# One queue for all transfers of the attention stage, expert weights in pieces of 256 KB, and the order of the parts written anew

## The chip, the core and the metric

The kernel runs on one core of a Trainium2 chip. The metric is the device time of one execution in microseconds (us). The kernel before takes 458.43 us (median of 3 runs, 458.0 to 460.66). Engines: TensorE (PE; its weight loads are PEld), VectorE (DVE), ScalarE (ACT), GpSimd (POOL). Transfers are issued from a queue of SyncE (SP) and from ACT's own instruction stream (ACTq in the rows).

## The reference, cut to what matters

Three stages follow each other: attention with a hash mask over 16 heads (2 batches of 8), a soft mixture of 8 experts, and a feed-forward layer with a sigmoid gate.

```python
# attention, per head: q, k, v are 768 x 64; proj is 64 x 6
mask = bucket(q @ proj > 0)[:, None] == bucket(k @ proj > 0)[None, :]
scores = where(mask, (q @ k.T) / 8, -1e9)
attn = softmax(scores) @ v              # 16 heads -> x: 1536 x 512
# experts: phi 512 x 32, w1 8 x 512 x 1024, w2 8 x 1024 x 512
logits = x @ phi
slots = softmax(logits, axis=0).T @ x   # 32 slots, 4 per expert
slot_out = relu(slots @ w1[e]) @ w2[e]
x = softmax(logits, axis=1) @ slot_out
# feed-forward: w_in 512 x 2048, w_out 2048 x 512, both float64
h = x @ w_in
out = (h * sigmoid(1.702 * h)) @ w_out  # float32, 1536 x 512
```

## The kernel before, in words

**Attention** works head by head (n = 0 to 15). For each head: `raw.n` loads q and k (128 x 768, 384 KB) into one of two buffers, `raw0` for even heads and `raw1` for odd ones; `bits.n` (PE, L370) projects them, `bits2.n` (DVE, L359) makes the bucket code `Bt`, and `bits3.n` moves it in four transfers of 48 KB into rows of the operand tile `QK2`. `hi2`, `hi1`, `hq` (ACT) and `lo1`, `lo2` (ACT and DVE, L341 and L347) split q and k into a high and a low part. `a.n.i` (PE L428, DVE L435) finds the row maxima, `mr.n` (PE, DVE) turns them into a row, and `ms.n` stores it (3 KB) into `QK2`. Then `c` (L478) and `s` (L486) make a block of scores on PE, ACT takes the exponential (L487) into `P`, POOL sums (L495), and `av` (L501) multiplies by v, which `v.n` loads (192 KB). The buffer of `raw.n` comes free when the last `lo2.(n-2)` has read it. The heads overlap: while one head's scores are made, the maxima of the next and the codes of the one after are under way.

Between them run parts of the later stages: `win.j` loads a 16th of w_in (512 KB), `w1.j` to `w3.j` narrow it to float32 in the one tile `wn`, and `w4.j` stores it to DRAM (256 KB, `win32`). `we.i` loads expert tile i (1 MB) for i = 0 to 13 into 14 reserved tiles, which nothing uses before. `spin` and `idle` are matmuls without a use that keep PE busy at the start.

**The order** is written out by hand: the string ATTENTION lists the parts (`c.3.2.0` is part c, head 3, key block 2, query half 0), a loop (L681 to L683) records them in that order, and each engine and queue does its own instructions strictly in that order, waiting where data or a buffer is not ready. A part does not wait for its turn in the string on another engine: SP runs ahead until one of its own instructions has to wait. MISC and XROWS assign buffers to parts in order of use.

**Queues before.** SP's queue carries the loads `raw`, `v`, `win`, `phi`, the moves `bits3` and the stores `ms` of heads 1 to 14. ACT's stream carries the 14 loads `we` (L205), the 16 stores `w4` (L656) and `ms.15` (L468), each between its computing instructions. Transfers share eight completion semaphores in turn, so that each one also waits for the one issued eight before it.

**After attention** the loads of expert tiles 14 to 31 stand in SP's queue (`more`, L730), the first nine of them (14 to 22) into memory that the attention stage gives back, the others into tiles that become free as `expert_in` (L935) and the loop at L975 use up experts 0, 1 and so on; then the tiles of w_out and of the narrowed w_in. The feed-forward stage (L1162 on) is one long row of matmuls.

Of the kernel before, what the change touches and what calls it, by code (L numbers as in the profile page):

```python
# [42 lines left out]
idle.0 hi1.0.0 spin.6 hi2.0.1 bits.0 lo.0.1 hi2.0.0 code.1.1 spin.2 code.1.0 code.0.0 hq.0 code.0.1 a0.0 bits.1 a0.5
a0.3 a0.4 lo.0.0 spin.1 a0.2 a0.1 hi1.0.1 a0.9 spin.1 a0.8 a0.6 c.0.0.0 raw.2 bits2.1 bits.2 hi2.1.0 mred.0 hi2.1.1
a0.10 mr0.0 a0.11 hi2.2.0 a0.7 bits3.1 mr1.0 lo.1.1 bits2.2 spin.1 hi2.2.1 spin.1 hi1.1.0 c.0.3.0 hi1.1.1 mred.1
s.0.0.0 a.1.0 spin.1 s.0.3.0 c.0.1.0 spin.1 vs.0 mr0.1 mr1.1 c.0.1.1 lo.1.0 w1.0 raw.3 v.1 a.1.1 c.0.2.0 spin.1 spin.1
s.0.1.0 p.0.1.0 s.0.1.1 spin.1 bits3.2 s.0.2.0 a.1.2 spin.1 c.0.4.0 spin.3 p.0.2.0 s.0.4.0 c.0.4.1 c.0.3.1 a.1.5
s.0.4.1 s.0.3.1 c.0.0.1 s.0.0.1 lo1.2.1 w2.0 hq.1 spin.2 c.0.5.1 a.1.4 c.0.2.1 w3.0 s.0.2.1 vs.1 av.0.0 av.0.1 p.0.1.1
a.1.3 c.0.5.0 s.0.5.1 hq.2 av.0.2 a.2.3 p.0.3.0 s.0.5.0 mr.1 av.0.3 c.1.0.0 lo2.2.1 w4.0 a.2.0 bits.3 win.1 p.0.4.0
av.0.4 hi2.3.0 ms.1 w1.1 hi2.3.1 bits2.3 a.2.1 s.1.0.0 bits3.3 w2.1 av.0.5 avo.0 p.0.2.1 c.1.0.1 p.0.3.1 s.1.0.1  # L50
p.0.4.1 a.2.2 mp.1 p.0.5.1 c.1.1.0 p.0.5.0 s.1.1.0 c.1.1.1 s.1.1.1 c.1.2.0 p.1.1.0 w3.1 s.1.2.0 c.1.3.0 s.1.3.0 w4.1
win.2 lo1.2.0 a.2.4 v.2 av.1.0 p.1.2.0 c.1.3.1 c.1.2.1 lo2.2.0 hi1.2.1 a.3.5 s.1.2.1 raw.4 we.0 av.1.1 s.1.3.1 c.1.4.0
p.1.1.1 a.2.5 p.1.2.1 w1.2 s.1.4.0 c.1.5.1 p.1.3.1 w2.2 av.1.2 mr.2 mp.2 ms.2 c.1.5.0 a.3.0 s.1.5.0 w3.2 s.1.5.1
bits.4 c.1.4.1 a.3.4 s.1.4.1 c.2.0.0 c.2.1.0 s.2.1.0 s.2.0.0 p.1.3.0 vs2.0 hi2.4.0 lo1.3.0 hq.3 c.2.0.1 vs.2 p.1.4.1
w4.2 bits2.4 win.3 s.2.0.1 a.3.3 av.1.3 av.1.4 p.1.5.1 c.2.2.0 p.1.4.0 c.2.1.1 bits3.4 p.1.5.0 lo1.3.1 a.3.1 nom.1
s.2.2.0 lo2.3.0 s.2.1.1 hi2.4.1 p.2.1.0 av.1.5 avo.1 c.2.3.1 hi1.3.1 a.3.2 c.2.2.1 s.2.2.1 c.2.3.0 s.2.3.0 sum.0 v.3
we.1 a.4.1 s.2.3.1 p.2.2.0 nom.0 av.2.0 lo2.3.1 av.2.1 av.2.2 w1.3 av.2.3 c.2.4.0 w2.3 we.2 p.2.1.1 mr.3 mp.3 c.2.4.1
s.2.4.1 c.2.5.0 raw.5 p.2.2.1 s.2.4.0 p.2.3.0 ms.3 w3.3 xtok.0 a.4.3 rec.0 s.2.5.0 we.3 c.2.5.1 s.2.5.1 xp.0 c.3.0.0
a.4.0 hi1.4.1 av.2.4 hi2.5.0 p.2.4.0 p.2.5.0 av.2.5 xn.0 bits.5 w4.3 lo1.4.0 c.3.1.0 p.2.3.1 p.2.4.1 s.3.1.0 bits2.5
bits3.5 a.4.5 s.3.0.0 c.3.0.1 s.3.0.1 win.4 xtok.1 avo.2 p.3.1.0 hq.4 raw.17 c.3.2.0 s.3.2.0 lo2.4.0 lo1.4.1 c.3.1.1  # L60
p.2.5.1 s.3.1.1 a.4.4 av.3.0 lo2.4.1 p.3.2.0 we.4 c.3.2.1 s.3.2.1 xp.1 c.3.3.0 hi2.5.1 a.4.2 xn.1 c.3.3.1 s.3.3.1
raw.6 vs.3 s.3.3.0 phi av.3.1 av.3.2 p.3.3.0 c.3.4.0 a.5.5 p.3.1.1 mp.4 p.3.2.1 s.3.4.0 c.4.4.0 c.3.4.1 s.3.4.1 mr.4
p.3.3.1 xT.0.0 c.3.5.0 s.3.5.0 a.5.0 lo1.5.0 p.3.4.1 bits.6 bits2.6 c.3.5.1 w1.4 c.4.2.0 ms.4 a.5.1 s.4.4.0 s.3.5.1
p.3.5.1 v.4 s.4.2.0 lo2.5.0 av.3.3 hi2.6.1 p.3.4.0 av.3.4 av.3.5 w2.4 hi1.5.1 a.5.2 bits3.6 c.4.1.0 avo.3 c.4.0.0 we.5
c.4.0.1 s.4.0.0 s.4.0.1 s.4.1.0 p.3.5.0 w3.4 vs2.1 a.5.3 c.4.1.1 s.4.1.1 c.4.3.0 lo1.5.1 s.4.3.0 c.4.4.1 p.4.1.0
av.4.0 win.5 p.4.1.1 hq.5 av.4.1 xT.0.1 c.4.3.1 lo2.5.1 a.5.4 s.4.3.1 lg.0 hi2.6.0 raw.7 sum.1 v.5 a.6.0 mr.5 c.4.5.0
p.4.2.0 c.4.2.1 s.4.2.1 s.4.5.0 raw.16 p.4.2.1 s.4.4.1 p.4.3.1 w4.4 rec.1 a.6.1 c.4.5.1 ms.5 av.4.2 bits.7 w1.5 vs.4
bits2.7 av.4.3 hi1.6.1 s.4.5.1 w2.5 hi2.7.1 bits3.7 nom.3 nom.2 c.5.1.1 c.5.0.0 w3.5 we.6 p.4.3.0 a.6.4 p.4.4.1 vs.5
hi2.7.0 w4.5 p.4.5.1 av.4.4 av.4.5 a.6.2 v.6 c.5.1.0 s.5.1.0 s.5.0.0 xtok.2 xtok.3 s.5.1.1 c.5.2.0 s.5.2.0 xp.2 xn.2
a.6.3 xp.3 avo.4 c.5.0.1 s.5.0.1 vs2.2 c.5.2.1 lo1.6.1 p.4.4.0 win.6 xn.3 lo2.6.1 mp.5 c.5.4.0 lo1.6.0 p.4.5.0 s.5.2.1  # L70
s.5.4.0 c.5.4.1 a.6.5 s.5.4.1 p.5.1.0 lo2.6.0 p.5.2.0 av.5.0 av.5.1 av.5.2 hq.6 p.5.1.1 a.7.0 c.5.3.1 c.5.5.0 raw.8
s.5.5.0 c.5.3.0 p.5.2.1 s.5.3.0 mr.6 s.5.3.1 xT.1.1 c.5.5.1 w1.6 a.7.1 s.5.5.1 av.5.3 p.5.3.1 av.5.4 bits.8 p.5.4.1
hi2.8.0 bits2.8 av.5.5 vs.6 c.6.0.0 hi1.7.1 ms.6 a.7.5 s.6.0.0 p.5.3.0 c.6.0.1 c.6.1.0 s.6.1.0 xT.1.0 p.5.4.0 s.6.0.1
w2.6 c.6.1.1 p.5.5.1 a.7.2 w3.6 bits3.8 p.5.5.0 hi2.8.1 avo.5 c.6.2.0 s.6.1.1 s.6.2.0 c.6.3.0 lg.1 lo1.7.0 a.7.3
lo2.7.0 p.6.1.0 s.6.3.0 p.6.1.1 nom.5 p.6.2.0 sum.2 v.7 lo1.7.1 win.7 c.6.2.1 c.6.4.0 s.6.2.1 s.6.4.0 hq.7 lo2.7.1
w1.7 nom.4 a.7.4 raw.9 p.6.2.1 mp.6 av.6.0 w4.6 av.6.1 vs.7 av.6.2 a.8.5 c.6.4.1 s.6.4.1 c.6.5.0 c.6.3.1 s.6.3.1 mr.7
s.6.5.0 p.6.3.1 c.6.5.1 w2.7 s.6.5.1 a.8.0 p.6.3.0 av.6.3 hi2.9.1 p.6.4.1 we.7 w3.7 bits.9 av.6.4 bits2.9 hq.8 a.8.4
ms.7 c.7.0.0 rec.2 c.7.1.0 s.7.0.0 s.7.1.0 xtok.4 a.8.1 lo1.8.0 lo2.8.0 c.7.0.1 hi1.8.1 p.7.1.0 s.7.0.1 av.6.5 avo.6
p.6.4.0 c.7.1.1 lo1.8.1 mp.7 c.7.2.0 s.7.2.0 w4.7 a.8.3 win.8 av.7.0 xp.4 s.7.1.1 c.7.2.1 xn.4 s.7.2.1 p.6.5.0 a.8.2
p.6.5.1 av.7.1 hi2.9.0 xtok.5 p.7.2.0 c.7.4.0 c.7.3.0 lo2.8.1 bits3.9 s.7.4.0 a.9.1 s.7.3.0 c.7.3.1 raw.10 p.7.1.1  # L80
p.7.2.1 mr.8 s.7.3.1 w1.8 xp.5 av.7.2 c.8.0.0 c.7.5.0 xn.5 p.7.3.0 p.7.4.0 a.9.5 s.7.5.0 av.7.3 ms.8 s.8.0.0 a.9.4
p.7.3.1 xT.2.0 c.7.5.1 w2.8 v.8 c.8.3.0 s.8.3.0 w3.8 c.7.4.1 s.7.4.1 s.7.5.1 hi2.10.0 a.9.0 vs2.3 lo1.9.0 c.8.2.0
c.8.0.1 s.8.0.1 lo2.9.0 av.7.4 av.7.5 w4.8 p.7.4.1 bits.10 bits2.10 p.7.5.1 hi2.10.1 xT.2.1 mp.8 c.8.1.0 c.8.3.1 hq.9
bits3.10 s.8.1.0 avo.7 s.8.2.0 p.8.1.0 a.9.3 lg.2 lo1.9.1 p.7.5.0 c.8.1.1 nom.6 s.8.1.1 a.9.2 c.8.2.1 p.8.1.1 s.8.3.1
p.8.2.0 hi1.9.1 s.8.2.1 av.8.0 p.8.3.0 c.8.5.0 c.8.4.0 lo2.9.1 mp.9 win.9 s.8.4.0 s.8.5.0 a.10.3 mr.9 w1.9 w2.9
c.8.4.1 av.8.1 av.8.2 sum.3 s.8.4.1 p.8.2.1 v.9 c.8.5.1 raw.11 w3.9 we.8 a.10.1 s.8.5.1 vs.8 c.9.1.0 ms.9 p.8.3.1
# [1167 lines left out]
```

## Time and profile before

| | |
|---|---|
| median of the runs | 458.43 us (458.0 to 460.66) |
| profiled execution | 462.48 us, span 460.5 us |
| busy in the span | PE 96%, DVE 66%, ACT 62%, POOL 47% |
| attention stage | about 0 to 259 us |
| experts | about 259 to 300 us |
| feed-forward | about 300 to 460 us |
| transfers | 75 MB, mean 163 GB/s |

All times inside the execution are us from the start of the span. PE is called busy for as long as a matmul of it is under way, and these overlap, so that 96% says little; where it waited is seen in the idle time in front of an instruction. The chain of waits is followed back from the last instruction, so that a transfer in it is one for which everything else waited.

### The profile page before, as it was taken

To read this page: it belongs to the slowest core of one execution; us is meant where nothing else is said; L and a number is where in the kernel's file an instruction comes from. 1 tells how busy PE (TensorE), PEld (TensorE's weight loads), DVE (VectorE), ACT (ScalarE), POOL (GpSimd) and SP (SyncE) were. 2 spreads that over 40 slices of the span, in tenths; PEclk is the share of its full clock that TensorE was granted. 3 is DMA by queue.
4 is the path that set the end of the run, shared out by engine and by line. 5 is a ranking of instruction groups with operands and counts; after the bars stand their busy time and mean duration, and the time that the engine had idled before them with its cause. 6 is when DMAs were issued, how large, how long until landed. Compare 5 with 4: busy or idle time off the path is not lost.

```text
span 460.5 us, 7059 instructions
## 1 busy us (share of the span) xinstructions
...
## 2 busy tenths in 40 slices
...
GB/s 158 102 84 228 88 325 236 205 217 70 192 142 103 140 145 204 145 171 148 106 226 264 426 381 426 388 419 422 81 0 1 1 0 139 0 1 68 0 2 68
DMA packets 22023, 75.08 MB, mean 163 GB/s; under 512 B 3210, under 2 KB 8804, under 8 KB 16612
## 3 DMA queue, kind: packets, MB, share of 16 engines
...
q14 instruction: 16, 0.13, 0.1%
...
## 4 chain that ended last, share of the span: by engine, by line
PE 70%; DMA 15%; DVE 7%; ACT 5%; issue 2%; POOL 0%; SPq 0%; ACTq 0%; DVEq 0%; POOLq 0%
PE o L1130 28%; PE av L501 9%; PE b L478 6%; DMA raw<-in_qk 6%; DMA w<-in_w 6%; PE a L428 6%; PE b L486 6%; PE h L1102 2%; PE bp L370 2%; DVE MX L435 2%; DVE QK L347 2%; ACT P L487 1%; DMA QK<-mr 1%; PE xtp L583 1%; DMA win<-wn 1%
## 5 line engine op out<-in xcount | busy, mean ns | idle before, releaser
L495 POOL TENSOR_TENSOR Ps<-Ps,P 128x384 f32<-128x384 f32 x120 | 119.2, 1007 | 38.9 <-ACT P L487 36.3
L487 ACT ACTIVATE P<-b 128x384 f32<-128x384 f32 x192 | 87.1, 491 | 42.6 <-PE b L486 40.5
L1130 PE MATMUL o<-wh,ring 128*128 128x512 f32 x384 | 110.0, 395 | 0.6 <-DVE cT L893 0.6
L435 DVE TENSOR_REDUCE MX<-a 128x1 f32<-128x768 f32 x90 | 85.8, 953 | 30.0 <-PE a L428 28.0
L1130 PEld LDWEIGHTS o<-wh,ring 128*128 128x128 f32 x384 | 71.0, 188 | 15.6 <-issue 1.4
L501 PE MATMUL av<-P,v 128*64 128x384 f32 x384 | 74.2, 499 | 0.1
L478 PE MATMUL b<-QK 128*128 128x384 f32 x192 | 66.7, 381 | 0.4 <-ACT P L487 0.4
L1111 DVE TENSOR_TENSOR XH<-h,XH 128x384 f32<-128x384 f32 x64 | 35.3, 555 | 46.3 <-ACT XH L1107 46.3
L486 PE MATMUL b<-QK 89*128 89x384 f32 (+1 forms) x192 | 62.3, 359 | 0.9 <-DMA QK<-mr 0.8
L1130 PE MATMUL o<-wl,ring 128*128 128x512 f32 x192 | 55.3, 394 | 0.0
L1107 ACT ACTIVATE XH<-h 128x384 f32<-128x384 f32 x64 | 31.3, 491 | 29.8 <-PE h L1102 29.5
L478 PEld LDWEIGHTS b<-QK 128*128 128x128 f32 x192 | 35.5, 194 | 22.3 <-issue 10.8
L428 PE MATMUL a<-QK 88*128 88x384 f32 x180 | 49.7, 357 | 0.0
L1116 ACT CAST ring<-XH 128x384 fp32r<-128x384 f32 x64 | 32.7, 513 | 23.0 <-DVE XH L1111 21.8
L1130 PEld LDWEIGHTS o<-wl,ring 128*128 128x128 f32 x192 | 35.8, 188 | 10.5 <-issue 2.5
L501 PEld LDWEIGHTS av<-P,v 128*64 128x64 f32 x384 | 23.3, 136 | 29.1 <-issue 25.1
L495 POOL TENSOR_TENSOR Ps<-P,P 128x384 f32<-128x384 f32 x30 | 30.1, 1006 | 22.7 <-ACT P L487 22.7
L486 PEld LDWEIGHTS b<-QK 89*128 89x128 f32 (+1 forms) x192 | 36.8, 195 | 5.6 <-issue 3.6
L428 PEld LDWEIGHTS a<-QK 88*128 88x128 f32 x180 | 31.6, 194 | 10.5 <-DVE MX L435 5.7
L1121 DVE TENSOR_TENSOR ring<-XH,ring 128x384 fp32r<-128x384 f32 x64 | 37.2, 585 | 1.7 <-ACT ring L1116 1.4
L931 POOL TENSOR_TENSOR wl<-XH,wh 128x512 fp32r<-128x512 f32 x16 | 22.6, 1412 | 30.3 <-ACT wh L926 30.1
L347 DVE TENSOR_TENSOR QK<-raw,lo 64x384 fp32r<-64x384 f32 x56 | 30.9, 552 | 3.2 <-ACT lo L341 2.1
(171 smaller groups left out, 557.2 us busy)
## 6 DMA issues: line engine op xcount, KB each, us to landing
w<-in_w SPq DMA_DIRECT2D x18, 1024.0 KB, 8.0
w<-in_w ACTq DMA_DIRECT2D x14, 1024.0 KB, 4.8
...
wof<-in_w_out SPq DMA_DIRECT2D x7, 1024.0 KB, 17.4
...
win<-wn ACTq DMA_DIRECT2D x16, 256.0 KB, 4.2
...
win<-win SPq DMA_DIRECT2D x3, 1024.0 KB
```

The costliest lines, as they stand in the source:

```text
L347: V.tensor_tensor(out=QK1[n % 2][r, s, c], in0=raw[n][r, c], in1=lot[h][r, :].bitcast(F32), op=ALU.subtract)
L428: T.matmul(a[:, h, 0:HS], q2[0:88, 0, i * 128 : (i + 1) * 128], q2[0:88, 1, h * HS : (h + 1) * HS], start=True, stop=True,)
L435: V.tensor_reduce(out=MX[:, n % 2, i : i + 1], in_=a[:, :, 0:HS], axis=AX.XY, op=ALU.max)
L478: T.matmul(b, q1[:, 1, kt * 128 : (kt + 1) * 128], q1[:, 0, h * HS : (h + 1) * HS], start=True, stop=False)
L486: T.matmul(b, q2[rows, 1, kt * 128 : (kt + 1) * 128], q2[rows, 0, qs], start=False, stop=True)
L487: A.activation(out=Pt[n, kt][:, qs], in_=b, func=AF.Exp, scale=0.125)
L495: e.tensor_tensor(out=Ps[n][:, c], in0=Pt[n, 0][:, c] if kt == 1 else Ps[n][:, c], in1=Pt[n, kt][:, c], op=ALU.add)
L501: T.matmul(avp[n][64 * h : 64 * h + 64, :], vt[n][:, kt, :], Pt[n, kt][:, h * HS : (h + 1) * HS], start=kt == 0, stop=kt == KT - 1,)
L1111: V.tensor_tensor(out=gt[i], in0=hp[i], in1=gt[i], op=ALU.mult)
L1116: A.copy(out=gh[i], in_=gt[i])
L1121: (e or V).tensor_tensor(out=gl[i], in0=gt[i], in1=gh[i].bitcast(F32), op=ALU.subtract)
L1130: T.matmul(op[grp, t], u[i][:, t * 128 : (t + 1) * 128], w[wq][:, wi, :], start=f == 0 and j == 0, stop=f == NF - 1 and j == 2,)
```

## The change

- All transfers of the attention stage are issued in SP's queue: ACT issues none.
- Each expert tile 0 to 13 is loaded by four transfers of 256 KB (`we.i.0` to `we.i.3`), which stand apart from each other in the order. Tiles 14 to 31 are loaded as before, 1 MB at a time.
- ATTENTION and MISC are written anew. The parts are the same, with the same counts of instructions on PE, DVE and POOL; ACT has 31 fewer (its transfers), and SP issues 244 transfers where it issued 171.

```diff
-MISC = "0 1 1 0 1 1 0 1 0 0 1 0 1 0 ...
+MISC = "0 1 1 0 1 1 0 1 0 1 1 1 0 0 ...
 ATTENTION = """
-idle.0 hi1.0.0 spin.6 hi2.0.1 bits.0 lo.0.1 hi2.0.0 code.1.1 spin.2 ...
+hi2.0.0 idle.0 hi2.0.1 spin.6 bits.0 lo.0.1 code.1.0 hi1.0.0 code.1.1 ...
...
-    def load_expert(i):
-        wtile[i] = take(F32, f"w{i}")
-        (A if i < NWA else SP).dma_start(wtile[i], experts[i])
+    def load_expert(i, j=None):
+        if not j:
+            wtile[i] = take(F32, f"w{i}")
+        if j is None:
+            SP.dma_start(wtile[i], experts[i])
+        else:
+            SP.dma_start(wtile[i][:, j, :], experts[i][:, j, :])
...
     def mstore(n):
-        (A if n == NH - 1 else SP).dma_start(QK2[n % 3][88:89, 0, :].bitcast(F32), mxs[n][0:KT, :].bitcast(F32))
+        SP.dma_start(QK2[n % 3][88:89, 0, :].bitcast(F32), mxs[n][0:KT, :].bitcast(F32))
...
     def win4(j):
-        A.dma_start(win32[j % 4][:, j // 4, :], wn[j])
+        SP.dma_start(win32[j % 4][:, j // 4, :], wn[j])
```

The lines of the change stand six lower than those of before (L347 is L353, L435 is L441, L205 is L211 for a piece). Three places of the new order follow, before and after; a number behind a part's name is its head or tile, and the last number only tells buffers apart.

**SP's queue around the load of head 4** (`raw4`; `w0`, `w1` are expert tiles, `wif` a load of w_in, `Bt3` the four moves of head 3's code, `mr2` the store of head 2's maxima). Before:

```order
L468 DMA QK2_1_88<-mr1_345 1x6x128
L352 DMA QK2_0_94<-Bt3_373 32x384 x4
L306 DMA wif2_428<-in_w_in 128x1024
L301 DMA v2_436<-in_v 128x384
L295 DMA raw4_455<-in_qk 128x768
L468 DMA QK2_2_91<-mr2_485 1x6x128
```

And in the change:

```order
L474 DMA QK2_1_88<-mr1_357 1x6x128
L211 DMA w0_247<-in_w1 128x512
L358 DMA QK2_0_94<-Bt3_385 32x384 x4
L211 DMA w1_455<-in_w1 128x512
L676 DMA phs_67<-in_phi 128x128
L301 DMA raw4_463<-in_qk 128x768
L662 DMA win32_1_76<-wn1_335 128x512
L307 DMA v2_485<-in_v 128x384
L211 DMA w1_455<-in_w1 128x512
L474 DMA QK2_2_91<-mr2_483 1x6x128
```

`v2` now stands behind the load of head 4 and `wif2` further up, ahead of `mr1`; one piece of an expert and `phi` have come to stand just ahead of the load in the same queue.

**DVE between the last reader of head 2's buffer and the code of head 4** (the first row is `lo2.2`, which frees the buffer; the next row behind each fence is `bits2.4`, which needs head 4's load). Before:

```order
L347 TENSOR_TENSOR QK1_0_92<-raw2_174,lo2_0_430 64x384 x2
L435 TENSOR_REDUCE MX_103<-a3_5_449 128x1
L435 TENSOR_REDUCE MX_103<-a2_5_467 128x1
L228 SCALAR_TENSOR_TENSOR wp2_473<-wp2_473,wif2_428 128x512
L444 TENSOR_SCALAR mr2_485<-mtp2_483 6x128
L435 TENSOR_REDUCE MX_103<-a3_0_492 128x1
L235 SCALAR_TENSOR_TENSOR wn2_498<-wif2_428,wp2_473 128x512
L435 TENSOR_REDUCE MX_103<-a3_4_507 128x1
L517 TENSOR_REDUCE vs02_534<-v2_436 128x64
```

And in the change:

```order
L353 TENSOR_TENSOR QK1_0_92<-raw2_220,lo2_1_410 64x384 x2
L441 TENSOR_REDUCE MX_103<-a2_5_450 128x1
L441 TENSOR_REDUCE MX_103<-a3_4_470 128x1
L450 TENSOR_SCALAR mr2_483<-mtp2_481 6x128
L234 SCALAR_TENSOR_TENSOR wp2_468<-wp2_468,wif2_361 128x512
L441 TENSOR_REDUCE MX_103<-a3_5_505 128x1
L241 SCALAR_TENSOR_TENSOR wn2_513<-wif2_361,wp2_468 128x512
L441 TENSOR_REDUCE MX_103<-a3_3_518 128x1
L353 TENSOR_TENSOR QK1_1_95<-raw3_264,lo3_0_501 64x384 x2
L441 TENSOR_REDUCE MX_103<-a3_1_546 128x1
L353 TENSOR_TENSOR QK1_1_95<-raw3_264,lo3_1_543 64x384 x2
L523 TENSOR_REDUCE vs02_555<-v2_485 128x64
```

One more reduction and the four `lo2` of head 3 have come in between: 13 instructions stand there where 8 stood (a row with x2 counts twice).

**SP's queue at the end of the attention stage** (`w12` and up are expert tiles, `win32` the stores of the narrowed w_in, `mr15` the store of the last head's maxima). Before, where ACT issued `mr15`, `wn15` and `w13`:

```order
L306 DMA wif15_2650<-in_w_in 128x1024
L301 DMA v15_2712<-in_v 128x384
L205 DMA w14_2931<-in_w1 128x2048
L205 DMA w15_2933<-in_w1 128x2048
L205 DMA w16_2935<-in_w2 128x2048
```

And in the change:

```order
L312 DMA wif15_2670<-in_w_in 128x1024
L211 DMA w12_2558<-in_w1 128x512
L662 DMA win32_2_77<-wn14_2652 128x512
L211 DMA w13_2728<-in_w1 128x512
L474 DMA QK2_0_94<-mr15_2757 1x6x128
L211 DMA w13_2728<-in_w1 128x512 x3
L662 DMA win32_3_78<-wn15_2759 128x512
L209 DMA w14_2973<-in_w1 128x2048
L209 DMA w15_2975<-in_w1 128x2048
L209 DMA w16_2977<-in_w2 128x2048
L209 DMA w17_2979<-in_w2 128x2048
```

The tiles 14 and up now stand behind the store of the last maxima, three pieces of tile 13 and the last store of the narrowed w_in.

## Rows read from the trace of the kernel before

**Rows 1.** The page's first line, and the chain of waits by engine.

```profile
span 460.5 us, 7059 instructions
PE 70%; DMA 15%; DVE 7%; ACT 5%; issue 2%; POOL 0%; SPq 0%; ACTq 0%; DVEq 0%; POOLq 0%
```

**Rows 2.** Chain of waits in order of time: start us, length us, what.

```profile
39.54 7.55 DMA raw<-in_qk
105.64 3.14 DMA raw<-in_qk
209.73 5.51 DMA raw<-in_qk
240.40 3.57 DMA QK<-mr
268.60 0.86 PE hp L941 x8
280.74 17.93 DMA w<-in_w
```

**Rows 3.** Waits of PE: us in total, times, longest.

```profile
PE bp L370 <- DMA raw<-in_qk: 7.3, 5, 3.9
```

**Rows 4.** Timeline around the loads of heads 4 and 15: start us, us, engine.

```profile
38.36 1.12 DVE L347 TENSOR_TENSOR QK<-raw,lo 64x384 fp32r<-64x384 f32 x2
39.25 0.37 ACTq L205 DMA_DIRECT2D w<-in_w  x1
47.22 1.54 PE L370 MATMUL bp<-raw,prj 128*64 128x384 f32 x4 [3.92 <-DMA raw<-in_qk]
215.38 0.87 PE L370 MATMUL bp<-raw,prj 128*64 128x384 f32 x4 [1.91 <-DMA raw<-in_qk]
```

**Rows 5.** Stretches: busy us by engine, granted clock, DMA share, GB/s.

```profile
47.20:55.00 7.80, 7.78 (x29) 5.41 (x30) 3.24 (x4) 4.04 (x9) 3.83 (x4) 0.64 0.26 95
60.00:90.00 30.00, 28.34 (x164) 18.08 (x162) 23.49 (x38) 22.11 (x46) 19.88 (x21) 1.00 0.73 269
215.00:220.00 5.00, 4.62 (x18) 3.96 (x19) 2.36 (x3) 3.43 (x7) 3.21 (x4) 0.66 0.56 195
260.00:270.00 10.00, 9.65 (x95) 5.24 (x97) 3.86 (x14) 2.75 (x11) 0.00 (x0) 1.00 1.01 419
```

**Rows 6.** SP's queue: stores of the maxima of heads 2, 3, 13 and 14.

```profile
44.14 0.74 SPq L468 DMA_DIRECT2D QK<-mr  x1
63.12 0.75 SPq L468 DMA_DIRECT2D QK<-mr  x1
207.38 0.75 SPq L468 DMA_DIRECT2D QK<-mr  x1
225.93 0.75 SPq L468 DMA_DIRECT2D QK<-mr  x1
```

**Rows 7.** Groups of DVE instructions: busy us, mean ns, idle before.

```profile
L435 DVE TENSOR_REDUCE MX<-a 128x1 f32<-128x768 f32 x90 | 85.8, 953 | 30.0 <-PE a L428 28.0 <-PE mtp L442 0.6
L347 DVE TENSOR_TENSOR QK<-raw,lo 64x384 fp32r<-64x384 f32 x56 | 30.9, 552 | 3.2 <-ACT lo L341 2.1
L228 DVE SCALAR_TENSOR_TENSOR wp<-wp,wif 128x512 int32<-128x512 int32 x16 | 11.0, 686 | 3.1 <-ACT wp L224 3.1
L517 DVE TENSOR_REDUCE vs<-v 128x64 f32<-128x384 f32 x16 | 13.3, 829 | 1.1 <-PE vsp L523 1.1
```

**Rows 8.** Transfers by kind: count, KB each, median us from issue to landing.

```profile
w<-in_w ACTq DMA_DIRECT2D x14, 1024.0 KB, 4.8
win<-wn ACTq DMA_DIRECT2D x16, 256.0 KB, 4.2
QK<-Bt SPq DMA_DIRECT2D x60, 48.0 KB, 2.0
```

**Rows 9.** SP at the end of attention: three expert loads, and its wait.

```profile
248.62 1.82 SPq L205 DMA_DIRECT2D w<-in_w  x3
SPq L205 <- DMA win<-wn: 9.5, 1, 9.5
```

More of the change, by code (lines that the diff above doesn't have):

```diff
@@ L42 @@
 ATTENTION = """
[L43 to L86, printed above, removed]
-xtok.6 s.9.1.0 hi1.10.1 c.9.0.0 rec.3 c.9.0.1 p.8.4.1 lo1.10.1 lo2.10.1 s.9.0.1 s.9.0.0 c.9.1.1 a.10.0 hi2.11.1
```

121 lines of the change are left out of this document (84 added, 37 removed).

## The prediction

> **What bounds the kernel now.** I read the views in this order: the chain of waits by engine, the chain in order of time, the waits of PE, then timelines and stretches around the places where the chain leaves PE. By engine the chain is PE 70%, DMA 15%, DVE 7%, ACT 5% [rows 1]. Some 160 us of the PE share are the feed-forward row of matmuls, which the change does not touch. What it can touch is the attention stage, and the DMA entries of the chain there.
>
> In that stage two loads of q and k stand out: head 4's, 7.55 us on the chain from 39.54, and head 15's, 5.51 us from 209.73, where an undisturbed one (at 105.64) took 3.14 [rows 2]. PE waited for such loads 7.3 us in all, in five places, 3.9 at the longest [rows 3]: 3.92 us before head 4's projection at 47.22 and 1.91 before head 15's at 215.38 [rows 4]. The reader should then look at the clock: behind the first wait the granted clock is 0.64 from 47.20 to 55.00, behind the second 0.66 from 215 to 220 [rows 5]. Of its two levels, 1.2 and 2.4 GHz, that is the lower one for 0.72 and 0.68 of the stretch: PE had stood still just before, and then does part of its work at half speed.
>
> Why was head 4's load late? `lo2.2` freed its buffer at 39.48 (38.36 plus 1.12), and SP issued it at 39.54, so SP was not late; but ACT had issued a 1 MB expert load at 39.25 [rows 4], and the two shared the DMA engines.
>
> After attention the experts' loads are the chain up to 298.7 us [rows 2], and SP's queue alone moves 419 GB/s in 260 to 270 [rows 5].
>
> **The change, part by part.**
>
> *The two late loads.* Their price, measured where they stand. Head 4: 3.92 us idle, and 0.72 x 7.8 us = 5.6 us at half speed, half of it lost, 2.8; together 6.7. Head 15: 1.91, and 0.68 x 5 us = 3.4 us, half of it 1.7, less the 0.38 us in which PE was idle in that stretch anyway; together 3.3. Sum 10.0. A second measure, which has in it what later heads made good: from one store of maxima to the next it took 18.98 us (head 2 to 3) and 18.55 (13 to 14), against 144.26 / 10 = 14.43 for the ten in between [rows 6]. The excess is 4.55 + 4.12 = 8.7. I take 8.7, the smaller.
>
> Do they go? Two things speak for it. In SP's new queue `raw4` has nothing large close ahead of it (one piece of 256 KB and the 64 KB of `phi`), where `wif2` and `v2` preceded it and a 1 MB load ran beside it in ACT's queue; `v2` now comes behind. And the cover has grown: on DVE, between the freeing of the buffer and the code that needs the new load, stood four reductions, two narrowing steps and one `vs`, 4 x 0.953 + 2 x 0.686 + 0.829 = 6.0 us [rows 7]; now a fifth reduction and four `lo2` of 0.552 stand there too, 9.2 us. Counted in the same way, head 15's cover goes from 2 reductions, 2 narrowing steps and 2 `lo2`, 4.4 us, to 4 reductions, 2 narrowing steps and a `vs`, 6.0. A load of 3.14 us, or even of 5.5, fits under both.
>
> *New tight places.* The shortest covers of the new order, in the same count, are those of head 10 (2 reductions, 2 narrowing steps, one `vs`: 4.1 us) and head 11 (3 reductions, 2 `lo2`: 4.0). If the loads there take the 5.51 us of head 15's instead of 3.14, PE waits 1.5 us twice and may lose as much again in clock; if 3.14, nothing. Between 0 and 6 us; I take 1.0, since no 1 MB transfer can stand beside them any more and no expert piece stands close ahead of them.
>
> *The start.* The four moves of head 1's code are now issued ahead of head 2's load. Between nothing and the time that four issues take, at most 4 x 0.74 = 3.0 us if each is as long as that of a store of maxima [rows 6]; I take 0.5, since the new order also puts head 2's projection later.
>
> *ACT without transfers.* 31 issues (14 expert loads, 16 stores of `wn`, the last store of maxima) at the 0.37 us of the one at 39.25 [rows 4] are 11.5 us off ACT. ACT is 5% of the chain, 23 us, nearly all in the first 300: some 8%. So 0.9 is gained; nothing and the full 11.5 are the ends.
>
> *SP with 73 more issues.* At 0.37 each, 27 us in a stage of 259, on a queue that mostly waits. Cost nothing, covered by SP's waits; what lies behind a waiting instruction there is a rival below.
>
> *The last store of maxima.* From ACT it took 3.57 us on the chain [rows 2]; a move of SP's lands in 2.0 [rows 8]. At most 1.6; I take 0.5, since a 256 KB piece may stand just ahead.
>
> *The end of the stage.* Before, SP's loads of tiles 15 to 17 were issued from 248.62, and tile 15 had waited 9.5 us for the last store of `wn` to land [rows 9], 8.2 us after ACT issued the last maxima at 240.40 [rows 2]. Now that store goes out behind the maxima and three pieces, about 0.75 + 4 x 0.37 = 2.2 us later, and lands some 4.2 after that [rows 8]: tile 15 some 2 us earlier relative to the maxima. It buys nothing: the tiles beyond the ninth wait until the experts' first matmul (268.60 [rows 2]) frees tile 0, and the 30 us from there to the last load are set by the DMA rate. So the end moves with the attention stage, one for one.
>
> *Everything else* in the new order (the same matmuls, reductions and exponentials in another sequence): 0, with 5 us to either side, a third of a head.
>
> **Sum:** -8.7 + 1.0 + 0.5 - 0.9 - 0.5 = -8.6 us. The profiled execution took 462.5 us; 462.5 - 8.6 = 453.9. It is 4 us above the median of 458.4, though, and from the median the same sum gives 449.8. Part of the two waits may be the excess of that one execution, so I take the middle, **451.8 us**.
>
> **The rivals.**
>
> *A. The loads are late elsewhere.* One late load, with its clock, costs 8.7 / 2 = 4.3 us; two in the new order (heads 10 and 11, or 5 and 6, where the queue holds expert pieces) give back the gain: 458. For it: four pieces per head are on average 1 MB in the same queue, 2.5 us at 419 GB/s [rows 5]. Against it: the covers.
>
> *B. The small transfers stand behind the pieces: slower.* The store of the maxima and the four moves of the code are needed within the head; in one queue each waits for all that was issued ahead. Two pieces are 2 x 262 KB / 419 GB/s = 1.25 us; over 15 heads 18.8 us, against the 8.6 gained: 458.4 + 10.2 = 468.6. It decides where less than 0.74 + 2.0 + 1.25 = 4.0 us of PE work stand between the maxima's row and the first score that needs it. For it: the last store of maxima was waited for even before [rows 2]. Against it: that one was alone, and the pieces stand mostly behind the stores, not ahead. The Trainium skill (DMA: Bandwidth & Descriptors, section Queues, rings and completion order) says that every DMA engine takes turns between queues packet by packet, so that a small transfer in a queue of its own passes a large one. By that rule the change gives up such passing, which is this rival; the 7.55 against 3.14 us of head 4's load [rows 2] shows that passing was not free.
>
> *C. ACT's issues held up more than their own time.* Each sat in a stream that has exponentials behind it. If half of the 11.5 us was on the path rather than 8%, 4.9 us more go: about 447, and with the new sequence better by a few us, 444.
>
> *D. Pieces do not overlap.* A 256 KB store takes 4.2 us to land and 1 MB took 4.8 [rows 8]. If each piece had to land before the next, 56 of them are 235 us of SP's queue in a stage of 259 that also holds everything else: over 500 us. Against it: three loads were issued within 1.82 us [rows 9], and 419 GB/s are not reached without overlap. The Trainium skill (the same page, section Bandwidth) asks for at least 1 MiB per transfer, because each has a fixed cost; by it the pieces lose rate, and by these rows they do not where they follow each other.
>
> **How the numbers follow.** 1% is 4.6 us (below 453.8 is faster, above 463.0 slower), about what a measurement of this kernel can tell from no change. Forecast 0.52, between 447 and 455.5, of which 0.06 above 453.8; A 0.23; B 0.13; C 0.10; D 0.02. Faster 0.46 + 0.10 = 0.56, same 0.06 + 0.23 = 0.29, slower 0.15. The range reaches from C's end to A's, 443.5 to 460.5, and leaves out B, D and the tails of A and C, some 0.2.
>
> **What would show it.** Right: no entry of a head's load over 4 us on the chain after the first 30 us, no stretch of low granted clock between 30 and 250, all steps from one store of maxima to the next below 17 us, no transfer in ACT's stream, the experts' first matmul at about 260. A: such entries and dips, at other heads. B: PE waiting for `QK<-mr` or for the codes in many heads, a few tenths to 1 us each. C: steps of 14 us or less throughout. Wrong altogether if the steps grow evenly with none of these: then the new sequence itself is worse.

## The result, and the profile after

The changed kernel takes **454.54 us** (median of 4 runs, 454.49 to 455.07) where the kernel before, run beside it, took 459.55 (458.0 to 461.56): a ratio of **0.9891, 95% interval 0.9845 to 0.9937**, so 1.1% faster. The medians differ by 5.0 us. The two profiled executions differ by more, 462.48 us (span 460.5) against 454.51 (span 452.7), since the one before was 3 us slower than its kernel's median. Each kernel has now and then a slower execution; the ratios here leave these out, the medians in us do not.

The table splits the 7.8 us between the two spans at marks that both traces have: the issue of the stores of maxima of heads 1 and 15, the first matmul of the experts on the chain, and the landing of the last expert load there (its start plus its length).

| stretch | before | after | difference |
|---|---|---|---|
| start to the store of head 1's maxima | 30.81 | 35.38 | +4.6 |
| from there to head 15's | 209.59 | 196.36 | -13.2 |
| to the experts' first matmul | 28.20 | 27.59 | -0.6 |
| to the landing of the last expert load | 30.07 | 31.49 | +1.4 |
| the rest | 161.8 | 161.9 | 0 |

The first mark does not cut the same work in both orders: by the store of head 2's maxima (45.58, before 44.14) only 1.4 of the 4.6 us are left.

The page's first line, and the chain of waits by engine, of the changed kernel; it answers to [rows 1]:

```profile
span 452.7 us, 7086 instructions
PE 76%; DMA 12%; DVE 5%; ACT 3%; issue 2%; SPq 1%; ACTq 0%; DVEq 0%
```

DMA, DVE and ACT each have a smaller share, PE a larger one. The chain in order of time after 30 us (start, length, what), its two longest DMA entries ahead of the experts, and the experts; it answers to [rows 2]:

```profile
98.56 5.56 DMA raw<-in_qk
...
191.91 7.27 DMA wif<-in_w_in
...
259.33 0.86 PE hp L947 x8
...
272.94 17.88 DMA w<-in_w
```

One q/k load is still there, that of head 8, as long as head 15's was; but by the next view PE stood still no more than 0.4 us for any such load. PE's waits in the attention stage (total, times, longest), against [rows 3]:

```profile
PE a L421 <- DVE mx L428: 3.3, 3, 1.9
PE a L434 <- DMA QK<-Bt: 1.6, 2, 1.4
PE b L492 <- DMA QK<-mr: 0.4, 1, 0.4
PE bp L382 <- DMA raw<-in_qk: 0.4, 1, 0.4
PE bp L376 <- DMA raw<-in_qk: 0.3, 1, 0.3
```

The 7.3 us for q/k are 0.7. New at the top is a wait for DVE's reduction of head 0's maxima, at the start, and a small one for head 14's moves of signs. The stretches show what they did to TensorE (busy us by engine, then granted clock, DMA share, GB/s), against [rows 5]:

```profile
12.00:22.00 10.00, 8.65 (x30) 6.52 (x31) 5.63 (x11) 3.22 (x5) 4.24 (x4) 0.50 0.30 85
30.00:60.00 30.00, 29.57 (x156) 18.45 (x156) 22.70 (x33) 22.69 (x47) 22.13 (x25) 1.00 0.60 180
...
230.00:235.00 5.00, 4.67 (x30) 1.99 (x27) 3.77 (x7) 1.24 (x4) 4.70 (x5) 1.00 0.15 55
```

The lower level (0.64 and 0.66 before, in the middle of attention) is gone from there, and sits at 12 to 22 us instead, at 0.50: 1.2 of 2.4 GHz for the whole stretch. PE had stood still for 1.92 us just before:

```profile
11.89 0.69 PE L421 MATMUL a<-QK 88*128 88x384 f32 x1 [1.92 <-DVE mx L428]
```

And the DMA engines are nearly idle from 230 to 235, just before the stage that they limit. The stores of maxima of heads 2 and 3, against [rows 6]:

```profile
45.58 0.74 SPq L474 DMA_DIRECT2D QK<-mr  x1
60.48 0.74 SPq L474 DMA_DIRECT2D QK<-mr  x1
```

SP's wait for the last store of `wn`, against [rows 9]:

```profile
SPq L209 <- DMA win<-wn: 4.0, 1, 4.0
```

It was 9.5. The step from head 2's store of maxima to 3's is 14.9 us where it was 19.0. Over all 14 steps the mean is 14.03, before 14.97.

### The profile page after: what moved, and what is told of

Its sections match the earlier page's. It is cut to its first block, busy times and chain, and to the rows that moved or that the text cites. A ratio compares the mean times of both kernels' runs of the same rounds, so it can differ in the third digit from the quotient of the medians.

```text
span 452.7 us, 7086 instructions
## 1 busy us (share of the span) xinstructions
PE 435.9 (96%) x2411; PEld 295.6 (65%) x2411; DVE 306.9 (68%) x526; ACT 284.8 (63%) x578; POOL 216.4 (48%) x237
## 4 chain that ended last, share of the span: by engine, by line
PE 76%; DMA 12%; DVE 5%; ACT 3%; issue 2%; SPq 1%; ACTq 0%; DVEq 0%
PE o L1136 29%; PE av L507 11%; PE b L484 6%; PE a L434 6%; PE b L492 6%; DMA w<-in_w 4%; DMA wif<-in_w_in 4%; PE hp L947 3%; PE h L1108 2%; DMA raw<-in_qk 2%; PE bp L376 2%; DVE MX L441 1%; PE idle L186 1%; DMA win<-wn 1%; PE xtp L589 1%
## 5 line engine op out<-in xcount | busy, mean ns | idle before, releaser
L501 POOL TENSOR_TENSOR Ps<-Ps,P 128x384 f32<-128x384 f32 x120 | 118.6, 1005 | 14.7 <-ACT P L493 11.8
L441 DVE TENSOR_REDUCE MX<-a 128x1 f32<-128x768 f32 x90 | 85.6, 952 | 24.4 <-PE a L434 23.5
L507 PE MATMUL av<-P,v 128*64 128x384 f32 x384 | 71.3, 496 | 0.0
L484 PE MATMUL b<-QK 128*128 128x384 f32 x192 | 65.4, 373 | 1.0 <-ACT QK L334 0.4
L1122 ACT CAST ring<-XH 128x384 fp32r<-128x384 f32 x64 | 32.7, 513 | 23.2 <-DVE XH L1117 22.1
L484 PEld LDWEIGHTS b<-QK 128*128 128x128 f32 x192 | 35.2, 191 | 14.9 <-issue 6.5
L507 PEld LDWEIGHTS av<-P,v 128*64 128x64 f32 x384 | 24.5, 136 | 30.0 <-issue 26.0
L492 PEld LDWEIGHTS b<-QK 89*128 89x128 f32 (+1 forms) x192 | 35.6, 190 | 4.6 <-issue 3.8
L353 DVE TENSOR_TENSOR QK<-raw,lo 64x384 fp32r<-64x384 f32 x56 | 30.9, 552 | 2.7 <-ACT lo L347 1.5
```

The lines of the kernel that those rows point to most:

```text
L441: V.tensor_reduce(out=MX[:, n % 2, i : i + 1], in_=a[:, :, 0:HS], axis=AX.XY, op=ALU.max)
L484: T.matmul(b, q1[:, 1, kt * 128 : (kt + 1) * 128], q1[:, 0, h * HS : (h + 1) * HS], start=True, stop=False)
L492: T.matmul(b, q2[rows, 1, kt * 128 : (kt + 1) * 128], q2[rows, 0, qs], start=False, stop=True)
L501: e.tensor_tensor(out=Ps[n][:, c], in0=Pt[n, 0][:, c] if kt == 1 else Ps[n][:, c], in1=Pt[n, kt][:, c], op=ALU.add)
L507: T.matmul(avp[n][64 * h : 64 * h + 64, :], vt[n][:, kt, :], Pt[n, kt][:, h * HS : (h + 1) * HS], start=kt == 0, stop=kt == KT - 1,)
L1122: A.copy(out=gh[i], in_=gt[i])
```

## The experiments

My theory after this result: the gain is that of the new order, which takes the late q/k loads off PE's path, and the one queue is worth little by itself. The rivals: the queue alone does it (nothing large runs beside the small transfers any more), or the pieces do. The first four kernels cross these. Each ratio is to the kernel before, run in turn with it on the same chip.

**1. The queue alone.** The order of before, whole tiles, all in SP's queue.

```diff
-        (A if i < NWA else SP).dma_start(wtile[i], experts[i])
+        SP.dma_start(wtile[i], experts[i])
-        (A if n == NH - 1 else SP).dma_start(QK2[n % 3][88:89, 0, :].bitcast(F32), mxs[n][0:KT, :].bitcast(F32))
+        SP.dma_start(QK2[n % 3][88:89, 0, :].bitcast(F32), mxs[n][0:KT, :].bitcast(F32))
-        A.dma_start(win32[j % 4][:, j // 4, :], wn[j])
+        SP.dma_start(win32[j % 4][:, j // 4, :], wn[j])
```

> The order of before, untouched; only ACT's 31 transfers go to SP's queue, each expert tile still in one transfer of 1 MB. Theory 1 (the gain is the order's: longer covers over the loads of q and k): the two late loads keep their short covers, and 1 MB transfers now stand in the same queue as the small ones, so 457 to 464 us; head 4's load, which is issued just before the expert's, comes in time, others come late. Theory 2 (the gain is the queue's: no second stream beside the loads, no issues on ACT): 453 to 456 us, with steps from one store of maxima to the next below 14.4 us on average.

462.83 us, ratio 1.0045 (0.9992 to 1.0098): no gain. PE's waits say why. The first line is that of the kernel before, the others, against [rows 3], are from here:

```profile
PE b L486 <- DMA QK<-mr: 0.8, 1, 0.8
```

```profile
PE b L486 <- DMA QK<-mr: 6.8, 4, 3.5
PE bp L370 <- DMA raw<-in_qk: 2.3, 3, 1.6
PE a L428 <- DMA QK<-Bt: 1.6, 1, 1.6
```

The wait for q/k fell from 7.3 to 2.3: the megabyte that ran beside head 4's load is now issued behind it in the same queue. The wait for the rows of maxima rose from 0.8 to 6.8. In the worst place (3.5) SP issued a megabyte at 146.37 and the row behind it at 147.66, and the row was 6.25 us on its way:

```profile
147.66 6.25 DMA QK<-mr
```

That is rival B's mechanism, in the old order. The Trainium skill (DMA: Bandwidth & Descriptors, section Queues, rings and completion order) says that the DMA engines take turns between queues packet by packet. The 0.8 us of waits with two queues against 6.8 with one agree with it.

**2. The queue and the pieces, in the old order.** As 1, each of the first 14 experts in four pieces one behind another.

```diff
-        SP.dma_start(wtile[i], experts[i])
+        if i < NWA:
+            for j in range(4):
+                SP.dma_start(wtile[i][:, j, :], experts[i][:, j, :])
+        else:
+            SP.dma_start(wtile[i], experts[i])
```

> As the kernel with the order of before and all transfers in SP's queue, but each expert tile in four transfers of 256 KB issued one behind the other at the place of the one. Both theories: within 1.5 us of that kernel, since the same bytes stand ahead of the same transfers; 3 more issues of 0.4 us per tile on SP may add some tenths. If the size of a transfer itself counted, it would differ by more than 3 us.

471.49 us, ratio 1.0273 (1.0191 to 1.0356): cutting the same bytes in four costs some 9 us against experiment 1. SP's queue shows what one expert costs it (start, length, engine), first in experiment 1, then here:

```profile
69.57 0.43 SPq L205 DMA_DIRECT2D w<-in_w  x1
```

```profile
70.85 1.84 SPq L207 DMA_DIRECT2D w<-in_w  x4
```

PE's waits grew in all three kinds:

```profile
PE b L490 <- DMA QK<-mr: 9.9, 3, 4.2
PE bp L374 <- DMA raw<-in_qk: 4.7, 4, 3.1
PE a L432 <- DMA QK<-Bt: 3.0, 1, 3.0
```

The queue (packets, MB, share of 16 engines' span) and the pieces (count, KB, median us to landing), for experiment 11:

```profile
q1 hardware_dynamic: 28036, 74.64, 45.4%
w<-in_w SPq DMA_DIRECT2D x56, 256.0 KB, 5.4
```

**3. The order alone.** The new order and its pieces; expert pieces, stores of `wn` and the last row of maxima again from ACT.

```diff
-            SP.dma_start(wtile[i][:, j, :], experts[i][:, j, :])
+            A.dma_start(wtile[i][:, j, :], experts[i][:, j, :])
-        SP.dma_start(QK2[n % 3][88:89, 0, :].bitcast(F32), mxs[n][0:KT, :].bitcast(F32))
+        (A if n == NH - 1 else SP).dma_start(QK2[n % 3][88:89, 0, :].bitcast(F32), mxs[n][0:KT, :].bitcast(F32))
-        SP.dma_start(win32[j % 4][:, j // 4, :], wn[j])
+        A.dma_start(win32[j % 4][:, j // 4, :], wn[j])
```

> The order of the change, with the 56 pieces (but not the last, whole tiles), the 16 stores of the narrowed w_in and the last store of maxima issued by ACT again. Theory 1: the covers stay, so no late load of q and k; 453 to 457 us, with ACT's 73 issues (27 us at 0.37) costing 8 per cent of that, 2 us, and the places where moves of the code stand behind pieces relieved. Theory 2: the gain is gone, 458 us or more, with heads' loads over 5 us on the chain.

475.1 us, ratio 1.0345 (1.0268 to 1.0423): worse than before. My theory, that the order is enough, falls here, but not in attention. There the order does its work alone: the list of PE's waits has none for q/k any more, the stores of maxima of heads 1 to 15 take 201.44 us (before 209.59, after 196.36), and the experts start 3.3 us earlier than before. First this run, then the kernel before:

```profile
265.12 1.04 PE L947 MATMUL hp<-w,siT 128*32 128x512 f32 x8
```

```profile
268.42 1.04 PE L941 MATMUL hp<-w,siT 128*32 128x512 f32 x8
```

The loss comes behind that. SP's wait at the experts' loads:

```profile
SPq L209 <- DMA win<-wn: 23.2, 1, 23.2
```

The last transfer in ACT's stream (start, length, engine):

```profile
253.79 0.45 ACTq L662 DMA_DIRECT2D win<-wn  x1
```

What the new order puts late stands in ACT's stream behind its exponentials: the last store of `wn` goes out at 253.79 (in the changed kernel 234.65), SP waits 23.2 us for it with all later loads behind, and the first matmul behind the experts' (`c4p`) starts at 309.82 instead of 291.86.

**4. The new order and queue without the pieces.** One transfer of 1 MB at the place of each first piece.

```diff
         if not j:
             wtile[i] = take(F32, f"w{i}")
-        if j is None:
-            SP.dma_start(wtile[i], experts[i])
-        else:
-            SP.dma_start(wtile[i][:, j, :], experts[i][:, j, :])
+            SP.dma_start(wtile[i], experts[i])
```

> The order of the change and SP's queue alone, but each expert tile in one transfer of 1 MB at the place of its first piece. If pieces matter because small transfers stand behind them (the prediction's rival B as a mechanism): a small transfer behind a tile waits up to 1.9 us longer (0.75 MB at 419 GB/s); with some 5 of 14 tiles just ahead of something urgent, 456 to 461 us. If the covers are long enough for 1 MB too: 453.5 to 455.5 us.

451.03 us, ratio **0.9836 (0.9764 to 0.9907)**. Its median is the lower, though the interval overlaps that of the changed kernel. Its chain of waits by engine:

```profile
PE 82%; DVE 7%; DMA 5%; ACT 3%; issue 1%; SPq 0%; ACTq 0%; DVEq 0%
```

Of PE's waits for DMA in attention one is left:

```profile
PE b L489 <- DMA QK<-mr: 0.6, 1, 0.6
```

This kernel and that of experiment 1 differ by the order alone: 0.9836 against 1.0045. So the gain comes from the order and the queue together; the pieces bring nothing on top. In the old order they cost 2.3%, in the new one, which spreads them, less than can be told apart. One kernel of the cross was not run, the new order with whole tiles issued by ACT; that the order needs the queue is shown with pieces only.

**5. What head 4's load was late for.** The kernel before, with one expert load moved.

```diff
-raw.4 we.0 av.1.1
+raw.4 av.1.1
-bits2.4 win.3 s.2.0.1
+bits2.4 win.3 we.0 s.2.0.1
```

> The kernel before with one step moved: the load of expert 0 (1 MB, ACT's queue) is issued after the store of head 3's projected rows instead of right behind head 4's q/k load. If the megabyte that runs beside it is what made head 4's load late (the 7.55 us on the chain at 39.5 and part of the 7.3 us that PE's matmuls of signs waited for q/k in the whole stage), that load lands in 3 to 4 us, PE's waits for q/k fall by 3 to 4 us and the time falls by 3 to 7 us (interval of the ratio below 1). If the stall came from the point at which SP issues the load (head 4's buffer free too late), the load is as late as before and the time stays within 1%.

456.63 us, ratio 0.9959 (0.9925 to 0.9992): some 2 us, less than the 3 to 7 of the first expectation and inside the 1% of the second. PE's waits in attention:

```profile
PE a L428 <- DMA QK<-Bt: 3.5, 1, 3.5
PE bp L370 <- DMA raw<-in_qk: 1.2, 1, 1.2
```

The timeline at the new place, ACT's queue and PE:

```profile
49.77 0.58 ACTq L205 DMA_DIRECT2D w<-in_w  x1
58.58 0.98 PE L428 MATMUL a<-QK 88*128 88x384 f32 x2 [3.51 <-DMA QK<-Bt]
```

And the chain between the two:

```profile
50.77 7.57 DMA QK<-Bt
```

The load of q/k went out at 41.92 and no longer held PE up (its projection started at 45.94 and had not waited for it); the four moves of head 4's signs, 192 KB in all, met the megabyte instead and took 7.57 us. The stall changed its victim, with the same length to 0.02 us [rows 2]. This shows the mechanism that the prediction named for head 4, and why moving the megabyte to this place repairs little: what stands beside it is late there too. The equal lengths are chance.

For head 15's load, the other late one [rows 2], no megabyte was to blame: in the kernel before, ACT issued none between 198.90 and 222.71, and in the middle of that load (209.73 to 215.24) the DMA engines stood idle (in the order of [rows 5]):

```profile
212.50:213.30 0.80, 0.80 (x7) 0.14 (x2) 0.69 (x2) 0.78 (x3) 0.80 (x2) 1.00 0.00 0
```

**6. The start.** The changed kernel, with the first weight's narrowing moved out of head 0's reductions.

```diff
-a0.7 w1.0 w2.0 hi1.1.0
+a0.7 hi1.1.0
-mred.0 a.1.0 mr0.0 lo.1.0
+mred.0 a.1.0 w1.0 w2.0 mr0.0 lo.1.0
```

> The changed kernel with the two narrowing steps of the first projection weight (ACT wif, DVE wp) moved from among head 0's maxima reductions to just ahead of head 0's transposed maxima. If these steps are what made the start 4.6 us longer than before (PE's 1.9 us wait for the maxima at 11.9 and the granted clock of 0.50 to 0.80 behind it), the first store of maxima comes back from 35.4 to 31 to 33 us and the time falls by 2 to 4.5 us. If it is the place of head 2's q/k load (issued 13.9 instead of 10.4) or the four moves of signs ahead of it, the store stays at 34 to 36 us and the time within 1 us.

453.75 us, ratio 0.9882 (0.9834 to 0.993), as the changed kernel. PE's 1.92 us pause at 11.89 became 0.79 at 13.18, yet head 1's store came at 35.19:

```profile
7.02 1.55 PE L376 MATMUL bp<-raw,prj 128*64 128x384 f32 x4 [0.65 <-DVE QK L365]
13.18 0.69 PE L421 MATMUL a<-QK 88*128 88x384 f32 x1 [0.79 <-DVE mx L428]
```

The first of these lines shows that PE was slow in this execution anyway: the four matmuls of head 1's signs took 1.55 us, and 0.87 in those of before and after. So this run can't say how much of the 4.6 us the pause is. Experiment 12 has the same edit and 0.87 us for these matmuls: there head 1's store came at 33.59, in experiment 4, which differs by this edit alone, at 35.26. That is 1.7 us, in one execution of each.

**7. Head 0's maxima in the old order**, in the changed kernel (the buffers in MISC follow):

```diff
-a0.0 a0.4 ... a0.7 w1.0 w2.0 ... a0.1 ... a0.9 ... a0.2 a0.5 a0.6 ... a0.3 ... a0.10 a0.11 ... a0.8 ... mred.0 a.1.0 mr0.0
+a0.0 a0.5 ... a0.3 ... a0.4 ... a0.2 ... a0.1 a0.9 a0.8 ... a0.6 ... mred.0 a0.10 mr0.0 a0.11 ... a0.7 mr1.0 ... mred.1 s.0.0.0 a.1.0 mr0.1 mr1.1 lo.1.0 w1.0 w2.0 w3.0
```

> The changed kernel with head 0's maxima in the order of the kernel before: the six score tiles of the first half first, its reduction and its transposed maxima ahead of the last two or three tiles, and the first projection weight's two narrowing steps behind both. Nothing else moves. If the start's 4.6 us come from the twelve tiles being done in an order in which the first half is complete last (first exponential on ACT at 22.9 us, before at 18.6), the first exponential comes at 18.5 to 20.5, the first store of maxima at 31 to 33.5 instead of 35.4, and the time falls by 1.5 to 4 us. If the start is bound by TensorE's granted clock alone (0.50 from 12 to 22 us in the changed kernel, full from 5 us in the kernel before), the store stays at 34 us or later when the clock is low up to 20 us, whatever the order. If the time lost at the start is hidden later by waits that shrink, the store comes earlier and the time stays within 1 us.

456.61 us, ratio 0.9989 (0.9958 to 1.002): it loses what the changed kernel had gained. The first exponential did come early; then DVE took the narrowing steps ahead of head 1's maxima (timeline of ACT, DVE and PE):

```profile
18.23 0.49 ACT L490 ACTIVATE P<-b 128x384 f32<-128x384 f32 x1 [0.47 <-PE b L489]
21.16 0.70 DVE L231 SCALAR_TENSOR_TENSOR wp<-wp,wif 128x512 int32<-128x512 int32 x1 [1.54 <-ACT wp L227]
...
23.50 0.88 PE L431 MATMUL a<-QK 88*128 88x384 f32 x2 [2.25 <-DVE MX L438]
```

The stretch behind it:

```profile
24.00:30.00 6.00, 5.27 (x20) 4.76 (x19) 2.60 (x4) 2.03 (x4) 1.00 (x1) 0.50 0.64 210
```

PE paused for 2.25 us, the granted clock behind that was 0.50, and head 1's store came at 37.64, 2.3 us later than in the changed kernel. The pause followed the narrowing steps to their new place, as it stood at their old one: DVE waits there for ACT's half of them, with the maxima behind.

**8. Head 14's moves ahead of two pieces**, in the changed kernel, where PE waited 1.39 us for them at 199.97. There they were issued at 192.39, behind two pieces, a store of `wn` and the load `wif` that took 7.27 us:

```profile
191.91 0.38 SPq L312 DMA_DIRECT2D wif<-in_w_in  x1
192.39 2.47 SPq L358 DMA_DIRECT2D QK<-Bt  x4
```

```diff
-c.12.2.1 bits3.14 s.12.0.1
+c.12.2.1 s.12.0.1
-bits2.14 ms.12 hi2.14.0
+bits2.14 ms.12 bits3.14 hi2.14.0
```

> The changed kernel with the four moves of head 14's signs issued on SP right behind head 12's store of maxima, ahead of two pieces of an expert, a store of projected rows and the load of the next projection weight, behind which they stood before. If small transfers that stand behind large ones in SP's queue cost the 1.4 us that PE waited for these signs at 200.0, the wait goes and the time falls by 1 to 2 us; if another wait (the maxima on DVE) takes its place, the time stays within 0.5 us.

456.95 us, ratio 0.9941 (0.9907 to 0.9976): no gain, if anything a loss against the changed kernel. The granted clock of its trace is 0.85 nearly throughout, so the trace can't be laid beside the others, and what took the place of that wait stays open.

**9. The last expert ahead of the last row of maxima**, in the changed kernel.

```diff
-we.13.0 ... ms.15 ... we.13.1 ... we.13.2 ... we.13.3
+we.13.0 we.13.1 we.13.2 we.13.3 ... ms.15
```

> The changed kernel with the last three pieces of expert 13 issued right behind its first, so ahead of the wait for head 15's store of maxima, which the prediction said buys nothing because the experts' stage starts when attention ends. If the end of the stage is bound by the transfers (DMA moved only 55 GB/s while SP stood at that store, and above 400 after it), the experts end 1.5 to 2 us earlier and so does the kernel. If it is bound by attention's end, nothing changes (within 0.5 us), or the store of maxima behind three more pieces makes head 15 later by up to 1 us.

453.02 us, ratio 0.9886 (0.9846 to 0.9926), not to be told from the changed kernel by time. In its trace the DMA engines moved 246 GB/s from 230 to 235 where the changed kernel moved 55, and from the start of the experts' first matmul to that of `c4p`, the first behind the experts, it took 30.96 us (259.80 to 290.76) instead of 32.71 (259.15 to 291.86):

```profile
230.00:235.00 5.00, 4.68 (x31) 1.53 (x29) 4.54 (x8) 1.39 (x4) 4.76 (x6) 1.00 0.70 246
```

So the stage's end followed its transfers, by 1.75 us in these two executions; the row of maxima came 0.8 us later (232.52).

**10. Experiments 4 and 7 together.**

> The changed kernel with both edits that looked good: each expert in one transfer of 1 MB at the place of its first piece (451.0 us alone) and head 0's maxima in the order of the kernel before. If the two gains add, 447 to 450 us, a ratio of 0.975 to 0.98; if the start is not on the path, 450 to 452 us, as the one edit alone.

452.84 us, ratio 0.9918 (0.989 to 0.9946): the gains do not add. By its ratio it is behind experiment 4 alone (0.9836), as 7 is behind the changed kernel, though here the intervals overlap.

**11. Why pieces cost: four pieces by partitions**, in experiment 2's kernel.

```diff
-                SP.dma_start(wtile[i][:, j, :], experts[i][:, j, :])
+                SP.dma_start(wtile[i][32 * j : 32 * j + 32], experts[i][32 * j : 32 * j + 32])
```

> The kernel before with all transfers in SP's queue and each expert in four transfers of 256 KB one behind another, cut by partitions (32 partitions with 8 KB each) instead of by columns (128 partitions with 2 KB each, which took 471.5 us against 462.8 for the whole megabyte). If the 2 KB rows made the pieces dear, this runs like the whole megabyte: 461 to 465 us. If the number of transfers did it (SP's issue of 0.46 us each, 1.8 us for four, and one more completion each), this runs like the other pieces: 469 to 473 us. If 32 partitions reach fewer DMA engines, it is slower than both.

488.85 us, ratio 1.0711 (1.0661 to 1.0762), slower than both. The queue and the pieces, and then PE's waits, against experiment 2:

```profile
q1 hardware_dynamic: 22660, 74.64, 48.5%
w<-in_w SPq DMA_DIRECT2D x56, 256.0 KB, 6.1
```

```profile
PE b L490 <- DMA QK<-mr: 10.3, 3, 4.2
PE bp L374 <- DMA raw<-in_qk: 8.1, 5, 3.6
PE a L432 <- DMA QK<-Bt: 6.0, 2, 4.6
```

Longer rows thus do not make the pieces cheap: with rows of 8 KB they land later (6.1 us, against 5.4 by columns) and hold the DMA engines longer, 48.5% of 486.4 us = 235.9 against 45.4% of 473.3 = 214.9, and 45.4% of 461.2 = 209.4 for whole tiles. Why is not shown. And since this cut has a price of its own, it does not clear the rows of 2 KB: what of the 9 us by columns is theirs, what SP's time to issue, stays open.

**12. The best version found.** Experiments 4 and 6 together.

> The changed kernel with each expert in one transfer of 1 MB at the place of its first piece (451.0 us alone) and the two narrowing steps of the first projection weight moved to just ahead of head 0's transposed maxima, which took PE's longest pause out of the start (1.92 us down to 0.79) but little time (453.8 us alone). If the pause and the low granted clock from 12 to 22 us behind it cost what they seem to, 448.5 to 450 us and a ratio to the kernel before of 0.978 to 0.982; if head 0's chain of maxima on DVE sets the start whatever TensorE does, 450 to 452 us, as with the one edit alone.

450.11 us, ratio **0.9853 (0.9804 to 0.9901)**, with head 1's store at 33.59. It is faster than the kernel before. Its median is 4.4 us below the changed kernel's, taken on another occasion, but the intervals of the two ratios overlap, and from experiment 4 alone it can't be told.

## Why the prediction was right

**The sum held, its terms less well.** The execution profiled before took 462.5 us and the sum made 453.9 of it; the one after took 454.5. Between the marks of the table, +4.6 at the start is offset by -13.2 in the heads. With head 2's store as the first mark, where the two orders compare better, the start is +1.4 (forecast 0.5), the heads -10.1 (-8.6, with the new tight places and ACT's share), the way to the experts -0.6 (-0.5) and the end of the stage +1.4 (0). These misses have both signs, and that they nearly cancel is luck. The time put on record was 451.8, between the sum from that execution and the sum from the median; the measured 454.54 lies above 453.8, in the part of the range to which the prediction gave 0.06.

- *The two late loads*, -8.7. Right in place: PE's waits for q/k went from 7.3 to 0.7 us, the dips of the granted clock are gone from the middle of attention, and the two long steps went from 19.0 and 18.6 to 14.9 and 11.5. For head 4's load the mechanism is right too; experiment 5 showed the megabyte to be the cause. For head 15's the prediction named no cause, and what held it up stays open. Its reading also left out a third long load on the chain, head 5's (5.71 us from 61.66), for which PE waited 0.23: the length of a load on the chain is not its price. And its covers were counted on DVE, 6.0 and 4.4 us, where PE stood still already 3.8 us behind the issue of head 4's load and 3.7 behind that of head 15's (its 3.3 us for head 15's wait and clock add up to 3.2). What it had not seen is that the whole gain needs both edits: the queue alone moves the wait to the rows of maxima (experiment 1), the order alone leaves the last store of `wn` in ACT's stream (3).
- *New tight places*, +1.0 for heads 10 and 11. Nothing was lost there: the one long q/k load on the chain is head 8's, 5.56 us, and PE's waits of that kind are 0.7 us in all. The small wait came for head 14's signs instead, 1.4.
- *The start*, +0.5 with 3.0 as its upper bound: **mis-sized**, it measured +1.4 at head 2's store (+4.6 at head 1's), and not for the reason given. I had priced SP's four moves and not looked at what else the new order puts there: the first weight's two narrowing steps among head 0's reductions. The trace shows PE's 1.92 us pause and a clock of 0.50 from 12 to 22. The 4.6 us are not one execution's chance: with this start head 1's store came at 34.99 to 35.57 in the traces of the changed kernel and experiments 3, 4 and 9, with the old one at 30.57 to 31.35 in those of before and experiments 1, 2 and 11, and at 33.23 in that of 5 (last section). Moving the steps brought back 1.7 us at head 1's store and as much at head 2's (43.77 in 12 against 45.44 in 4), which is all that was left there.
- *ACT without its 31 transfers*, -0.9, and *SP's 73 more*, 0. Experiment 1 takes the same 31 off ACT for SP. Its new waits could hide a gain, but the steps that none of them touches are as long as before: from the store of head 11 to 12, 12 to 13 and 14 to 15 they are 14.5, 11.8 and 14.5 us in both. So rival C, that ACT's issues hold up far more than their time, is out. The second term was wrong in kind: 42 of the 73 issues are the pieces', and in the old order cutting in pieces costs some 9 us (2).
- *The last store of maxima*, -0.5: PE's wait for it (0.8) is gone, and the stretch from it to the experts' first matmul shrank by 0.6.
- *The end of the stage*, "one for one": not quite. From the experts' first matmul to the last load it took 31.49 us, before 30.07: three pieces of the last expert stood behind SP's wait for head 15's row while DMA idled at 55 GB/s. With them ahead, the stage was 1.75 us shorter (9).
- *The rest of the new order*, 0 with 5 either side. The heads gained 13.2, and the listed stalls are 8.7 of them. Of the other 4.5, 3.1 are the step from head 1's store to head 2's (10.2 us, before 13.3) and so belong with the start's 4.6. No run takes the remaining 1.4 apart.

**The signs named beforehand.** Held: no low clock between 30 and 250, no transfer in ACT's stream, the experts' first matmul at 259.33. Missed: one q/k load over 4 us on the chain (98.56), and two steps of 17.1 and 17.5 us (heads 4 to 5 and 7 to 8) where all were to be below 17.

**The rivals.** A happened once, at the price of 0.3 us of PE's time. B is real: 6.8 us of waits for the rows in the old order (1), one place of 1.4 us in the new, which puts the pieces mostly behind the small transfers. The price of 18.8 us for 15 heads did not come due. C is out. D in its strong form is out, as pieces overlap: three were issued within 2.05 us in the changed kernel. But its rule of thumb was the better guide than my rows: the Trainium skill (DMA: Bandwidth & Descriptors, section Bandwidth) asks for at least 1 MiB in a transfer, and the 256 KB pieces lost 2.3% in experiment 2, against whole tiles in the same order and queue.
